# Clamping and shifting weight words in PSUM, and running the last group of a feed-forward layer by token block

## The chip, the cores and the metric

The kernel runs on one core of a Trainium2 chip. The time is the device time of one execution, in microseconds (us); the profile is that of one execution on the same core. Engines are named as in the profile: PE is TensorE's matmul (PEld its weight load), DVE is VectorE, ACT is ScalarE, POOL is GpSimd, SP is the engine whose queue issues the loads.

## The reference

Attention over 2 batches, 8 heads, 576 tokens and 64 dimensions a head, with rotary embedding and a softmax, and after it two feed-forward layers on 1152 tokens of 512 columns. The weights are float64.

```python
x = attention(rotate(q), rotate(k), v)         # 1152 x 512
h = np.maximum(x @ w_in, 0.0)                  # 512 x 2048
x = (h * h @ w_out).astype(np.float32)         # 2048 x 512
a = x @ w_a                                    # 512 x 1536
b = x @ w_b
out = (a * b @ w2_out).astype(np.float32)      # 1536 x 512
```

## The kernel before

**Attention.** Eight pairs of heads, nine blocks of queries each. A block's scores are made on PE (`emit_S`, line 202), their maximum on DVE, the exponential on ACT (`emit_exp`, line 217), then transposes and the product with V on PE. All eight PSUM banks are in use: pool `ps` has the tags `s` (two slots of two banks), `t` and `av` (two slots of one bank each). The last pair's product is evacuated when the feed-forward stage starts.

**Feed-forward stage.** A matmul in full float32 is made of three in a rounded format (`three`, lines 390 to 392): weight high part by activation high part, high by low, low by high. So every weight and every activation is split into a high part (a cast) and a low part (a subtraction). Tokens run in three blocks of 384 (`NTB`, `TB`). In the first layer 16 blocks of 128 hidden columns are taken in groups of four (`G`). `unit1(f, n)` makes block f for token block n: 12 matmuls into a PSUM bank, the relu on ACT (line 416), then `gated`: the product v on DVE (line 408, one operand in PSUM, one in SBUF), a cast on ACT (line 409), a subtraction on POOL (line 410). `out1(g, m, n)` sums a group's four blocks: 12 matmuls (they carry the lines 390 to 392 too, as y<-g,w_o), then an add into an accumulator on DVE, and for the last group a split of the result into `yb`, the input of the second layer. In the second layer `unit2` makes two products and gates them, `out2` sums them and stores.

PSUM results of this stage go round the three tags of `ps` in turn (`bank`, line 384): six banks, of each `s` slot only the first half.

**Weights.** `prep_weight` (line 63) is called for each of 68 weight blocks ahead of the first step that wants it. SP loads 512 float64 words a partition (`raw`, two slots). ACT scales the high words and bends negative ones (lines 75 and 76, into `cl`, two slots in SBUF). DVE shifts the low words right by 29 into `bits` (line 77), clamps `cl` (line 78), and shifts `cl` left by 3 and ors the two (line 79). `bits` (two slots in SBUF) is then the float32 weight. ACT casts it to the high part in `w` (line 81), POOL subtracts to make the low part (line 82). `w` has 14 slots, three of which lie outside of what attention occupies. Loads, casts and steps of later weights run ahead of their use as far as the slots allow.

**Order.** `steps` (line 475 on) lists the units: for the first group all four blocks by token block; then, for each group, the rest of its units by block f with n inside, the first block of the next group, and the sums. The last group's sums run by token block. Each engine runs its own instructions in an order fixed when the program is built, so the order within an engine need not be that of the code, but an instruction that waits holds all behind it on its engine.

Of the kernel before, what the change touches and what calls it, by code (L numbers as in the profile page):

```python
# [7 lines left out]
F32 = mybir.dt.float32  # L8
# [5 lines left out]
ALU = mybir.AluOpType  # L14
AX = mybir.AxisListType

P = 128
# [4 lines left out]
NTB = 3  # L22
KC = 4
NF1 = 16
NF2 = 12
G = 4
LT = 3
DM = 512
NWT = 14
NWA = 3  # L30
BANKS = ("t", "av", "s")


@with_exitstack
def attention_moe_moe2_kernel(ctx: ExitStack, tc: tile.TileContext, qk, rope, vm, vt, ident_in, sel_in, w_in, w_out, w_a, w_b, w2_out, out):
    nc = tc.nc
    act, dve, pool, pe = nc.scalar, nc.vector, nc.gpsimd, nc.tensor
# [6 lines left out]
    tmp = ctx.enter_context(tc.tile_pool(name="tmp", bufs=1))  # L44
# [8 lines left out]
    def psum_s(name):  # L53
        return ps.tile([P, 2, 512], F32, tag="s", name=name)

    def psum_1(tag, name):
        return ps.tile([P, 512], F32, tag=tag, name=name)
# [5 lines left out]
    def prep_weight(key):  # L63
        st = raw.tile([P, DM], I64, tag="raw", name=f"raw_{key[0]}{key[1]}")
        nc.sync.dma_start(out=st, in_=src_of[key[0]][key[1]])
        w = wpools[int(len(W) % NWT >= NWA)].tile([P, 2, DM], F32R, tag="w", name=f"w_{key[0]}{key[1]}")
        W[key] = w
        words = st.bitcast(I32).rearrange("p (n two) -> p n two", two=2)
        low = words[:, :, 0]
        highf = st.bitcast(F32).rearrange("p (n two) -> p n two", two=2)[:, :, 1]  # L70
        cl = tmp.tile([P, DM], F32, tag="cl", bufs=2, name=f"cl_{key[0]}{key[1]}")
        bits = tmp.tile([P, DM], I32, tag="bits", bufs=2, name=f"bits_{key[0]}{key[1]}")
        clb = cl.bitcast(I32)

        act.activation(cl, highf, AF.Copy, scale=REBIAS)
        act.activation(cl, cl, AF.Prelu, alpha=TURN)
        dve.tensor_scalar(out=bits, in0=low, scalar1=29, scalar2=None, op0=ALU.logical_shift_right)  # L77
        dve.tensor_scalar(out=cl, in0=cl, scalar1=-HI * TURN, scalar2=HI, op0=ALU.max, op1=ALU.min)
        dve.scalar_tensor_tensor(out=bits, in0=clb, scalar=3, in1=bits, op0=ALU.logical_shift_left, op1=ALU.bitwise_or)
        val = bits.bitcast(F32)  # L80
        act.copy(w[:, 0, :], val)
        pool.tensor_tensor(out=w[:, 1, :], in0=val, in1=w[:, 0, :].bitcast(F32), op=ALU.subtract)  # L82
# [1 line left out]
    src_of = {"i": w_in, "o": w_out, "a": w_a, "b": w_b, "2": w2_out}  # L84
    W = {}

    ps = ctx.enter_context(tc.tile_pool(name="ps", bufs=2, space=bass.MemoryType.PSUM))
    attn = ExitStack()
    a1 = attn.enter_context(tc.tile_pool(name="a1", bufs=1))
    a2 = attn.enter_context(tc.tile_pool(name="a2", bufs=2))  # L90
    pp = attn.enter_context(tc.tile_pool(name="pp", bufs=5))
# [254 lines left out]
    for i in range(NB + LT):  # L346
# [19 lines left out]
        if p + 1 < NPAIR:  # L366
            n = p + 1
# [11 lines left out]
    wpools.append(ctx.enter_context(tc.tile_pool(name="wb", bufs=NWT - NWA, reuse_waits="tile")))  # L379
    accp = ctx.enter_context(tc.tile_pool(name="accp", bufs=1, reuse_waits="tile"))  # L380

    banks = [0]

    def bank(name):
        tag = BANKS[banks[0] % len(BANKS)]
        banks[0] += 1
        return psum_s(name)[:, 0, :] if tag == "s" else psum_1(tag, name)

    def three(dst, wh, wl, mh, ml, first, last):
        pe.matmul(dst, wh, mh, start=first, stop=False)  # L390
# [21 lines left out]
    def unit1(f, n):  # L412
        h = bank(f"h{f}_{n}")[:, 0:TB]
        proj(h, W["i", f], xb[n])
        r = g2.tile([P, TB], F32, tag="r", name=f"r{f}_{n}")
        act.activation(r, h, AF.Relu)
        gated(("g", f), n, h, r, f"1_{f}")

    def unit2(f, n):
        a = bank(f"a{f}_{n}")[:, 0:TB]  # L420
        proj(a, W["a", f], yb[n])
        r = g2.tile([P, TB], F32, tag="r", name=f"s{f}_{n}")
        act.copy(r, a)
        b = bank(f"b{f}_{n}")[:, 0:TB]
        proj(b, W["b", f], yb[n])
        gated(("ab", f), n, b, r, f"2_{f}")
# [48 lines left out]
    steps = []  # L475
    N1, N2 = NF1 // G, NF2 // G
    steps += [(unit1, f, n) for n in range(NTB) for f in range(G)]
    for g in range(N1):
        if g:
            steps += [(unit1, g * G + f, n) for f in range(1, G) for n in range(NTB)]  # L480
        if g + 1 < N1:
            steps += [(unit1, (g + 1) * G, n) for n in range(NTB)]
        if g < N1 - 1:
            steps += [(out1, g, m, n) for m in range(KC) for n in range(NTB)]
        else:
            steps += [(out1, g, m, n) for n in range(NTB) for m in range(KC)]
    for g in range(N2):
        steps += [(unit2, g * G + f, n) for f in range(0 if g == 0 else 1, G) for n in range(NTB)]
        if g + 1 < N2:
# [3 lines left out]
    for fn, *a in steps:  # L493
        if fn is unit1:
            keys = [("i", a[0])]
        elif fn is unit2:
            keys = [("a", a[0]), ("b", a[0])]
        else:
            keys = [("o" if fn is out1 else "2", a[0] * G + k) for k in range(G)]
        for key in keys:  # L500
            if key not in W:
                prep_weight(key)
        fn(*a)
# [66 lines left out]
```

## Time and profile before

| what | us |
|---|---|
| median of 3 runs (628.09 to 630.75) | 628.31 |
| the profiled execution | 628.47 |
| its span in the trace | 626.7 |
| PE busy | 591.8 |
| DVE busy | 352.1 |
| ACT busy | 322.4 |
| POOL busy | 267.7 |

The span runs from the first to the last instruction of the profiled execution; a row's start is counted from the span's start. [...]

### The profile page before, as it was taken

To read this page: it belongs to the slowest core of one execution; us is meant where nothing else is said; L and a number is where in the kernel's file an instruction comes from. 1 tells how busy PE (TensorE), PEld (TensorE's weight loads), DVE (VectorE), ACT (ScalarE), POOL (GpSimd) and SP (SyncE) were. 2 spreads that over 40 slices of the span, in tenths; PEclk is the share of its full clock that TensorE was granted. 3 is DMA by queue.
4 is the path that set the end of the run, shared out by engine and by line. 5 is a ranking of instruction groups with operands and counts; after the bars stand their busy time and mean duration, and the time that the engine had idled before them with its cause. 6 is when DMAs were issued, how large, how long until landed. Compare 5 with 4: busy or idle time off the path is not lost.

```text
span 626.7 us, 8927 instructions
## 1 busy us (share of the span) xinstructions
PE 591.8 (94%) x3368; PEld 523.3 (84%) x3368; DVE 352.1 (56%) x550; ACT 322.4 (51%) x685; POOL 267.7 (43%) x278
## 2 busy tenths in 40 slices
PE   0699999999999979999999979999999999999998
PEld 0667665666659968999999979999998999889986
DVE  5977677765528894855766676653441545221122
ACT  2577776787646777652563464455534644102200
POOL 4557656622127772652653452344450454302210
PEclk9999999999999999999999999999999999999999
DMA  7665756562004442411421331142221421000012
GB/s 244 179 189 140 208 167 191 120 188 57 18 1 152 150 144 94 158 59 53 134 68 69 93 109 35 66 130 73 67 68 69 134 68 68 0 1 1 0 52 100
DMA packets 20678, 61.41 MB, mean 98 GB/s; under 512 B 3337, under 2 KB 3721, under 8 KB 19739
## 3 DMA queue, kind: packets, MB, share of 16 engines
q1 hardware_dynamic: 20635, 60.85, 31.6%
q8 instruction: 26, 0.43, 0.3%
q14 instruction: 17, 0.14, 0.1%
HBM read 48.16 MB, written 2.36 MB: 81 GB/s over the span
## 4 chain that ended last, share of the span: by engine, by line
PE 62%; DVE 12%; issue 9%; ACT 6%; DMA 5%; POOL 4%; SPq 0%; ACTq 0%; DVEq 0%; POOLq 0%
PE s L202 8%; PE av L314 7%; PE t L272 5%; PE a L392 4%; PE b L392 4%; PE a L390 4%; PE b L390 4%; PE a L391 4%; PE b L391 4%; PE o L466 4%; PE o L465 4%; PE o L464 4%; POOL w_i L82 2%; DVE bits_o L77 2%; PE y L391 1%
## 5 line engine op out<-in xcount | busy, mean ns | idle before, releaser
L410 POOL TENSOR_TENSOR g<-v,g 128x384 fp32r<-128x384 f32 x84 | 94.9, 1130 | 142.6 <-ACT g L409 140.2
L409 ACT CAST g<-v 128x384 fp32r<-128x384 f32 x84 | 42.8, 509 | 82.4 <-DVE v L408 82.1
L202 PE MATMUL s<-sk 128*128 128x288 f32 x336 | 66.0, 327 | 19.6 <-DVE sk L180 14.5
L202 PEld LDWEIGHTS s<-sk 128*128 128x128 f32 x336 | 49.8, 200 | 38.4 <-DVE sk L180 14.5
L390 PE MATMUL y<-g,w_o 128*128 128x384 f32 x192 | 65.7, 342 | 8.4 <-DVE v L408 4.0
L211 DVE TENSOR_REDUCE st<-s 128x1 f32<-128x576 f32 x72 | 53.7, 752 | 33.8 <-PE s L202 33.6
L391 PE MATMUL y<-g,w_o 128*128 128x384 f32 x192 | 65.0, 339 | 0.9 <-POOL g L410 0.9
L392 PE MATMUL y<-g,w_o 128*128 128x384 f32 x192 | 64.8, 338 | 0.0
L390 PE MATMUL h<-x,w_i 128*128 128x384 f32 x192 | 64.3, 335 | 0.2 <-DVE v L408 0.2
L392 PE MATMUL h<-x,w_i 128*128 128x384 f32 x192 | 64.1, 334 | 0.0
L391 PE MATMUL h<-x,w_i 128*128 128x384 f32 x192 | 64.1, 334 | 0.0
L217 ACT ACTIVATE P<-s,st 128x576 f32<-128x576 f32 x72 | 53.6, 745 | 11.9 <-DVE st L211 11.8
L314 PE MATMUL av<-PT,V 128*64 128x384 f32 (+1 forms) x256 | 53.1, 426 | 0.0
L272 PE MATMUL t<-ident,P 128*128 128x128 f32 x288 | 46.5, 285 | 1.7 <-DVE PT L257 1.5
L392 PE MATMUL a<-yb,w_a 128*128 128x384 f32 x144 | 48.1, 334 | 0.0
L390 PE MATMUL a<-yb,w_a 128*128 128x384 f32 x144 | 48.1, 334 | 0.0
L391 PE MATMUL a<-yb,w_a 128*128 128x384 f32 x144 | 48.1, 334 | 0.0
L390 PE MATMUL b<-yb,w_b 128*128 128x384 f32 x144 | 48.1, 334 | 0.0
L391 PE MATMUL b<-yb,w_b 128*128 128x384 f32 x144 | 48.1, 334 | 0.0
L392 PE MATMUL b<-yb,w_b 128*128 128x384 f32 x144 | 48.1, 334 | 0.0
L390 PEld LDWEIGHTS y<-g,w_o 128*128 128x128 f32 x192 | 36.4, 190 | 11.4 <-DVE v L408 5.6
L466 PE MATMUL o<-w,g 128*128 128x512 f32 (+1 forms) x112 | 42.8, 382 | 0.0
(118 smaller groups left out, 1345.7 us busy)
## 6 DMA issues: line engine op xcount, KB each, us to landing
raw_i<-in_w_in SPq DMA_DIRECT2D x16, 512.0 KB, 3.4
raw_o<-in_w_out SPq DMA_DIRECT2D x16, 512.0 KB, 3.3
X<-in_qk SPq DMA_DIRECT2D x7, 1152.0 KB, 5.4
raw_a<-in_w_a SPq DMA_DIRECT2D x12, 512.0 KB, 3.2
raw_b<-in_w_b SPq DMA_DIRECT2D x12, 512.0 KB, 3.4
raw<-in_w_out SPq DMA_DIRECT2D x12, 512.0 KB, 3.4
sk<-hi_lo SPq DMA_DIRECT2D x14, 432.0 KB, 5.7
sk<-hi_lo SPq DMA_DIRECT2D x14, 288.0 KB, 5.9
```

The costliest lines, as they stand in the source:

```text
L202: pe.matmul(s[:, b, c:c + n], lhs, rhs, start=(m < 2), stop=(m >= len(mm) - len(cuts)), skip_group_check=(j == 8))
L211: dve.tensor_reduce(out=ST[p][:, 0, j:j + 1], in_=SP[i][:, :, 0:288], op=ALU.max, axis=AX.XY, negate=True)
L217: act.activation(pr[:, h, :].rearrange("p (b n) -> p b n", b=2), SP.pop(i)[:, :, 0:288], AF.Exp, bias=st[:, 0, j:j + 1], scale=1.0, accum_ ...
L272: pe.transpose(t[:, k * P:(k + 1) * P], flat[:, c0:c0 + P], ident)
L314: pe.matmul(AVT[p, r][half(h), 0:n], V[p][:, h, k, :], PT[p][:, h, k, q0:q0 + n], start=False, stop=(k == 3), skip_group_check=True)
L390: pe.matmul(dst, wh, mh, start=first, stop=False)
L391: pe.matmul(dst, wh, ml, start=False, stop=False)
L392: pe.matmul(dst, wl, mh, start=False, stop=last)
L409: act.copy(gt[:, 0, c], val)
L410: pool.tensor_tensor(out=gt[:, 1, c], in0=val, in1=gt[:, 0, c].bitcast(F32), op=ALU.subtract)
L464: pe.matmul(dst, gt[:, 0, c], w[:, 0, d], start=(k == 0), stop=False)
L466: pe.matmul(dst, gt[:, 1, c], w[:, 0, d], start=False, stop=(k == G - 1))
```

## The change

Four edits. In `prep_weight` the tile `cl` moves to a PSUM pool `mps` (two slots, one bank each); the list `mps` is filled before the first call, so every weight takes that branch. The clamp is now followed by a shift of `cl` in place, and the last DVE step shifts the raw low words and ors them with `cl`; the early shift of the low words into `bits` is gone. The pool `ps` is closed with attention, and all results of the feed-forward stage come from one tag `m` of `mps`, six slots of one bank. The pool's tiles wait for the tiles that they overlap, not for the whole pool before them (`reuse_waits="tile"`). And in the first layer's last group the units and the sums alternate by token block: units of block 0, units of block 1, sums of block 0, units of block 2, sums of block 1, sums of block 2.

```diff
+        if mps:
+            cl = mps[0].tile([P, DM], F32, tag="cl", bufs=2, name=f"cl_{key[0]}{key[1]}")
+        else:
+            cl = tmp.tile([P, DM], F32, tag="cl", name=f"cl_{key[0]}{key[1]}")
         clb = cl.bitcast(I32)

         act.activation(cl, highf, AF.Copy, scale=REBIAS)
         act.activation(cl, cl, AF.Prelu, alpha=TURN)
-        dve.tensor_scalar(out=bits, in0=low, scalar1=29, scalar2=None, op0=ALU.logical_shift_right)
         dve.tensor_scalar(out=cl, in0=cl, scalar1=-HI * TURN, scalar2=HI, op0=ALU.max, op1=ALU.min)
-        dve.scalar_tensor_tensor(out=bits, in0=clb, scalar=3, in1=bits, op0=ALU.logical_shift_left, op1=ALU.bitwise_or)
+        dve.tensor_scalar(out=clb, in0=clb, scalar1=3, scalar2=None, op0=ALU.logical_shift_left)
+        dve.scalar_tensor_tensor(out=bits, in0=low, scalar=29, in1=clb, op0=ALU.logical_shift_right, op1=ALU.bitwise_or)
...
-    ps = ctx.enter_context(tc.tile_pool(name="ps", bufs=2, space=bass.MemoryType.PSUM))
+    mps = []
     attn = ExitStack()
+    ps = attn.enter_context(tc.tile_pool(name="ps", bufs=2, space=bass.MemoryType.PSUM))
...
+    mps.append(ctx.enter_context(tc.tile_pool(name="mps", bufs=6, space=bass.MemoryType.PSUM, reuse_waits="tile")))

     def bank(name):
-        tag = BANKS[banks[0] % len(BANKS)]
-        banks[0] += 1
-        return psum_s(name)[:, 0, :] if tag == "s" else psum_1(tag, name)
+        return mps[0].tile([P, 512], F32, tag="m", name=name)
...
-        if g:
+        if 0 < g < N1 - 1:
             steps += [(unit1, g * G + f, n) for f in range(1, G) for n in range(NTB)]
...
         else:
-            steps += [(out1, g, m, n) for n in range(NTB) for m in range(KC)]
+            for n in range(NTB + 1):
+                if n < NTB:
+                    steps += [(unit1, g * G + f, n) for f in range(1, G)]
+                if n:
+                    steps += [(out1, g, m, n - 1) for m in range(KC)]
```

## Rows read from the trace of the kernel before

**Rows 1.** The page, part 1: busy us (share of the span) xinstructions.

```profile
PE 591.8 (94%) x3368; PEld 523.3 (84%) x3368; DVE 352.1 (56%) x550; ACT 322.4 (51%) x685; POOL 267.7 (43%) x278
```

**Rows 2.** What PE waited for, whole span: us in total, times, longest.

```profile
PE s L202 <- DVE sk L180: 14.5, 1, 14.5
...
PE y L390 <- DVE v L408: 4.0, 4, 1.4
...
PE t L272 <- DVE PT L257: 1.5, 1, 1.5
```

**Rows 3.** Timeline of PE: start, duration (us), engine, line, operation, out<-in, count.

```profile
185.86 0.44 PE L390 MATMUL h<-x,w_i 128*128 128x384 f32 x1
...
190.13 0.33 PE L390 MATMUL h<-x,w_i 128*128 128x384 f32 x1
```

**Rows 4.** Timeline of PE; in brackets the idle time before, and its releaser.

```profile
222.09 0.44 PE L390 MATMUL y<-g,w_o 128*128 128x384 f32 x1 [1.45 <-DVE v L408]
```

**Rows 5.** Timeline of DVE and PE, 371 to 379 us.

```profile
371.13 1.21 DVE L77 TENSOR_SCALAR bits<-raw 128x512 int32<-128x512 int32 x1
...
372.99 0.55 DVE L408 TENSOR_TENSOR v<-h,r 128x384 f32<-128x384 f32 x1
...
374.19 0.44 PE L390 MATMUL y<-g,w_o 128*128 128x384 f32 x1 [2.88 <-ACT g L409]
...
375.27 0.69 PE L391 MATMUL y<-g,w_o 128*128 128x384 f32 x1 [0.64 <-POOL g L410]
...
378.25 0.34 PE L391 MATMUL y<-g,w_o 128*128 128x384 f32 x1
```

**Rows 6.** Busy time by window: PE, PEld, DVE, ACT, POOL, then granted clock PEclk.

```profile
376.00:378.00 2.00, 2.00 (x8) 2.00 (x8) 0.65 (x2) 2.00 (x5) 1.40 (x2) 0.50 0.00 0
```

**Rows 7.** Timeline of DVE: the stage's 14th v, the last group's third.

```profile
230.89 0.54 DVE L408 TENSOR_TENSOR v<-h,r 128x384 f32<-128x384 f32 x1
...
361.03 0.55 DVE L408 TENSOR_TENSOR v<-h,r 128x384 f32<-128x384 f32 x1
```

**Rows 8.** Busy time by window of the shift, L77: window, DVE busy (count), PEclk.

```profile
0.00:187.00 187.00, 2.08 (x5) 1.00 0.51 143
...
187.00:231.50 44.50, 14.78 (x13) 1.00 0.43 142
```

**Rows 9.** The same of the clamp, L78.

```profile
0.00:187.00 187.00, 2.90 (x7) 1.00 0.51 143
...
187.00:231.50 44.50, 6.39 (x10) 1.00 0.43 142
```

**Rows 10.** The same of the shift-and-or, L79.

```profile
0.00:187.00 187.00, 3.42 (x5) 1.00 0.51 143
...
187.00:231.50 44.50, 12.69 (x12) 1.00 0.43 142
```

**Rows 11.** The same of v, L408.

```profile
187.00:231.50 44.50, 7.67 (x14) 1.00 0.43 142
```

**Rows 12.** Groups by line and shape, whole span: busy us, mean ns, idle before.

```profile
L257 DVE COPY PT<-t 128x512 f32<-128x512 f32 x15 | 10.2, 683 | 2.9 <-PE t L272 2.9
```

**Rows 13.** Tile cl_i, to 190 us: ns min/median/max, first and last start us.

```profile
L75 ACT ACTIVATE cl_i<-raw_i x5: 668/672/683, 73.3 to 131.8; 128x512 f32<-128x512 f32 x5
...
L76 ACT ACTIVATE cl_i<-cl_i x5: 617/642/660, 74.3 to 133.4; 128x512 f32<-128x512 f32 x5
...
L78 DVE TENSOR_SCALAR cl_i<-cl_i x5: 396/411/422, 80.6 to 136.0; 128x512 f32<-128x512 f32 x5
```

**Rows 14.** Busy time by window of all engines: PE, PEld, DVE, ACT, POOL.

```profile
187.00:231.50 44.50, 40.09 (x225) 38.16 (x223) 39.14 (x49) 30.95 (x62) 34.17 (x28) 1.00 0.43 142
```

**Rows 15.** The page, part 6: DMA issues, count, KB, median us to landing.

```profile
raw_i<-in_w_in SPq DMA_DIRECT2D x16, 512.0 KB, 3.4
```

**Rows 16.** Timeline of ACT: end of the first score slot's last softmax.

```profile
169.45 0.20 ACT L217 ACTIVATION_READ_ACCUMULATOR P<-s,st 128x1 f32 x1
```

**Rows 17.** Timeline of POOL: the last w_in weight's low half.

```profile
300.25 1.29 POOL L82 TENSOR_TENSOR w_i<-bits_i,w_i 128x512 fp32r<-128x512 f32 x1 [12.75 <-ACT w_i L81]
```

More of the change, by code (lines that the diff above doesn't have):

```diff
@@ L30 @@
 NWA = 3
-BANKS = ("t", "av", "s")
 @with_exitstack
@@ L70, in prep_weight @@
         highf = st.bitcast(F32).rearrange("p (n two) -> p n two", two=2)[:, :, 1]
-        cl = tmp.tile([P, DM], F32, tag="cl", bufs=2, name=f"cl_{key[0]}{key[1]}")
         bits = tmp.tile([P, DM], I32, tag="bits", bufs=2, name=f"bits_{key[0]}{key[1]}")
+        if mps:
+            cl = mps[0].tile([P, DM], F32, tag="cl", bufs=2, name=f"cl_{key[0]}{key[1]}")
+        else:
+            cl = tmp.tile([P, DM], F32, tag="cl", name=f"cl_{key[0]}{key[1]}")
         clb = cl.bitcast(I32)
@@ L380, in attention_moe_moe2_kernel @@
     accp = ctx.enter_context(tc.tile_pool(name="accp", bufs=1, reuse_waits="tile"))
-    banks = [0]
+    mps.append(ctx.enter_context(tc.tile_pool(name="mps", bufs=6, space=bass.MemoryType.PSUM, reuse_waits="tile")))
     def bank(name):
-        tag = BANKS[banks[0] % len(BANKS)]
-        banks[0] += 1
-        return psum_s(name)[:, 0, :] if tag == "s" else psum_1(tag, name)
+        return mps[0].tile([P, 512], F32, tag="m", name=name)
     def three(dst, wh, wl, mh, ml, first, last):
```

## The prediction

> **What bounds the kernel now.** I read the busy table first, then what TensorE (PE) waited for, then the PE timeline where those waits lie. PE is busy for 94% of the span [rows 1], so the change can be worth only PE's idle time and what a lower clock costs. Of the 34.9 us between busy time and span, 14.5 us are the start, before the first scores [rows 2], and 8 us more lie in the first 40 us and behind the last matmul; the change reaches none of these. Attention keeps one stop of 1.5 us, at 99 us [rows 2]. The feed-forward stage begins at 185.86 us [rows 3] and has two places where PE stops. From 215 to 246 us there are eight stops, 5.5 us in all (the largest is shown) [rows 4]. [...] A stop of 0.41 us at 288 us is the rest; layer two has none.
>
> Place one, 215 to 231 us. A unit of the first layer is 12 matmuls: 24 of them lie between the two matmul rows, 4.27 us, so about 2.1 us a unit [rows 3]. VectorE (DVE) must make v for each before its bank comes free. The 14th v starts at 230.89 us [rows 7]; its unit's matmuls ended near 185.9 + 14 x 2.1 = 215 us, so DVE is 16 us late. Six banks cover five further units, some 10.4 us; beyond that PE stops. DVE is full there: in 44.5 us the shift took 14.78 us, the clamp 6.39, the shift-and-or 12.69 and v 7.67 [rows 8 to 11], 41.5 us together. The three weight steps are that long only beside GpSimd (POOL) work. Before 187 us, where POOL has little to do, a shift took 2.08/5 = 0.42 us, a clamp 0.41, a shift-and-or 0.68; in the stretch they took 1.14, 0.64 and 1.06 [rows 8 to 10]. The v step, one operand in PSUM and one in SBUF, took 0.55 us in the midst of it [rows 11].
>
> Place two, 371 us. The last group's first sum has used three of its four gated blocks and waits for the fourth, whose v started at 372.99 us, behind weight steps of the second layer such as the shift of 1.21 us at 371.13 [rows 5]. That block's unit is two units ahead of the group's last, which ended at 369.6 us, so it ended near 365.4: DVE was 7.5 us late.
>
> **Part 1: clamp and shift in PSUM.** Per weight three DVE steps stay three, and all follow the second ScalarE (ACT) step; the shift on the low word, which could run early, is gone. The trace has no clamp that writes PSUM. The nearest row is the copy of 512 columns out of PSUM, 0.68 us on DVE [rows 12]; the floor is the quiet clamp, 0.41 us [rows 9], and the ceiling 0.64 to 1.14 us, if the waits beside POOL stay. I take 0.68 for clamp and shift, because operand place and size match, and 0.69 for the last step, its quiet value: 2.05 us a weight, against 2.84 in the stretch and 1.51 in quiet. With at most one operand in SBUF these should behave like v, which POOL never stretched. In the stretch: 12 weights x 2.05 = 24.6, plus 2.7 us for what was done ahead of 187 us and now isn't (two clamps and most of the fifth weight), plus 7.7 for v: 35.0 us instead of 41.5. DVE would be 16 - 6.5 = 9.5 us late, just inside the 10.4 us that banks cover. So the five stops released by DVE go (4.0 us [rows 2] and a short one of 0.2); of the other three (1.3 us, ACT and POOL last) I count a quarter. Gain 4.5 us, bounds 0 and 5.5. On ACT the two steps go to PSUM instead of SBUF; they took 0.67 and 0.64 us [rows 13], and I count no change, since ACT is busy 31 of the 44.5 us [rows 14].
>
> [...]
>
> The raw words are now held to the third DVE step instead of the first, so the next load on SP's queue is issued later by about two steps. Nothing else is queued on SP after the last attention load. One round of a raw slot becomes landing 3.4 [rows 15], ACT 1.3 [rows 13], DVE 2.05, some hand-overs: 7.1 us, for two slots 3.55 us a weight; before, 12 weights took 44.5 us, 3.7 us each [rows 10]. PE needs the ninth weight at 217 us and the 17th at 267; counted from 170 us that is 5.2 and 5.7 us a weight. Cost zero while a weight takes less; above, 9 us for each us of excess.
>
> **Part 2: PSUM anew.** Six banks rotate for sums as before; two now hold clamped words. Before, five weights (the clamps at 80.6 to 136.0 us [rows 13]) were made inside attention. Now none can be until attention gives banks back. I assume that slots are laid out in the order of first request, so that the two clamp slots fall on the first score slot, read last by the softmax that ended at 169.65 us [rows 16]; which slot it is the trace doesn't say. Then weight i0 is whole at 169.7 + 1.3 + 2.05 + 0.6 + 1.3, about 175 us, i1 at 177.5, i2, after its load, at 182.5 and i3 at 187; PE wants them at 185.9, 188, 190 and 192. Cost 0.5 us (0 to 2) for their ACT and DVE steps between attention's last ones. Inside attention, the steps that leave free some time: a shift of 0.42 us [rows 8] stands on DVE in the queue ahead of the 1.5 us stop [rows 2]. Gain 0.4 (0 to 1.5).
>
> **Part 3: the last group by token block.** PE's work is the same. The first sum now starts after six units instead of nine, and needs the third unit, not the seventh. With the lateness of before, that unit's v came at 361.0 us [rows 7]; behind v come a cast on ACT and POOL's subtraction, which at place two let the matmul start 2.3 us after v did (372.99 to 375.27 [rows 5]), so about 363.5. The sum wants it at about 365. Afterwards each block's sums (4 x 2.1 = 8.3 us of PE) stand between its last unit and its use. So both stops go, 2.88 + 0.64 us [rows 5]. And the clock: from 375.27 to 378.25 us [rows 5] nine matmuls took 2.98 us instead of 9 x 0.178 = 1.6, so 1.4 us more. Together 4.9 us (bounds 3 and 4.9). The three w_in weights are wanted within 6 us, not 19; the last of them was whole at 301.6 us [rows 17]. Their slots come free 5 to 17 us later, which delays three second-layer weights to about 376 us; PE needs those after 430.
>
> **Sum.** 628.3 - 4.5 - 4.9 - 0.4 + 0.5 = 619.0 us. The profiled execution took 628.47 us with a span of 626.7, the median is 628.31, so differences in the trace count one to one.
>
> **Rivals.**
> *Only part 3 pays.* DVE is relieved, but ACT or POOL (34 of 44.5 us busy [rows 14]) is late in its place, and the stops at 215 to 246 us stay: 628.3 - 4.9 = 623.4. For it: three stops there were released by those two. Against: these are the short ones. 0.15.
>
> *Clamp slots come free only at attention's end.* If the two banks are read until 186.4 us, i0 is ready for PE at 190.4, i2, whose load then starts at 189.8, at 197.3, and i3 at 199.4 instead of 192: 7.3 us lost, and about 1.4 us for the clock that such a stop cost at 374 us. 619.0 + 8.7 = 627.7, no change. 0.11.
>
> [...] 0.06.
>
> *Slower: weights are late.* Raw words, clamped words and bits have two slots each, all held longer. If one weight at a time goes round, 7.1 us each, the ninth comes at 170 + 64 = 234 instead of 217 us, 17 us late, and the 32nd at 397 instead of 386 plus those 17, no further loss. 619.0 + 17 = 636. It decides from 6.3 us a weight on, where 9 us eat the gain. Against it the pace of 3.7 us before. With orders on the engines that turn out worse in some such way, 0.12.
>
> **How the numbers follow.** The forecast, 616.5 to 622, has 0.56; the rivals 0.15, 0.11, 0.06 and 0.12. Up to 628 leaves out the last and the third; below 616.5 all stops of the feed-forward stage and the one in attention would have to go. Range 616.5 to 628. A measurement of this kernel tells 0.5%, 3.1 us, from no change: faster is below 625.2. Forecast and first rival with it 0.72 (0.71 and a little of the second), within 0.5% 0.16, slower 0.12.
>
> **What would show it.** Clamp and shift at 0.65 to 0.7 us each, the same beside POOL and away from it; no PE stop above 0.3 us between 210 and 246 us after the same count of units; no stop and no clock below 1.00 in the last group; the first feed-forward matmul within 1 us of 185.9, and no PE wait on a weight's ACT cast behind it. Wrong would be: DVE steps above 0.9 us, first clamps after 180 us, PE waiting for a weight's high or low half, or a new stop where the first block's sums begin.

## The result, and the profile after

| kernel (same chip) | median, us | runs, us | ratio to before, 95% interval |
|---|---|---|---|
| before | 628.85 | 628.09 to 630.75 | |
| changed | 621.0 | 620.45 to 622.08 | 0.9873 [0.9845, 0.9901] |

The change is worth 7.9 us; 9.3 were predicted, and 621.0 lies within the range. The profiled execution took 620.49 us with a span of 618.7, 7.98 us less than that of before. Two terms of the sum were far off, though, in opposite directions. That shows in the trace before any experiment.

The page of the changed kernel, part 1 (compare [rows 1]), and two of its costliest groups (line, engine, operation, out<-in, count, busy and mean ns, idle before). All lines of the weight and gating code lie one to three higher than before: copy L77, prelu L78, clamp L79, shift L80, last step L81, v L409.

```profile
PE 584.4 (94%) x3368; PEld 521.7 (84%) x3368; DVE 333.9 (54%) x550; ACT 322.1 (52%) x685; POOL 255.2 (41%) x278
...
L411 POOL TENSOR_TENSOR g<-v,g 128x384 fp32r<-128x384 f32 x84 | 85.3, 1018 | 136.7 <-ACT g L410 129.9
...
L391 PE MATMUL h<-x,w_i 128*128 128x384 f32 x192 | 65.5, 341 | 7.3 <-ACT w_i L83 7.3
```

What PE waited for in the changed kernel, whole span: us in total, times, longest (compare [rows 2]).

```profile
PE s L205 <- DVE sk L183: 15.0, 1, 15.0
PE h L391 <- ACT w_i L83: 7.3, 2, 6.2
PE s L205 <- ACT P L220: 5.4, 3, 4.0
PE r L250 <- DVE rows L260: 1.2, 2, 1.0
PE h L393 <- POOL w_i L84: 1.1, 2, 0.7
PE t L275 <- DVE PT L260: 0.8, 1, 0.8
```

The waits of sums on v [rows 2], at 222 us [rows 4] among them, and those on the cast and the subtraction behind a late v at 374 us [rows 5] are gone. In their place stands a wait that the kernel before didn't have: PE waits for the first weights of the feed-forward stage.

The timeline of ACT, DVE and PE there (start, duration, engine, line, operation, out<-in, count; in brackets the idle time before, and its releaser).

```profile
163.14 0.75 ACT L220 ACTIVATE P<-s,st 128x576 f32<-128x576 f32 x1
...
178.15 0.60 ACT L333 CAST x<-xf 128x192 fp32r<-128x192 f32 x2 [2.85 <-DVE xf L330]
...
180.76 0.35 ACT L333 CAST x<-xf 128x192 fp32r<-128x192 f32 x1 [1.22 <-DVE xf L330]
181.01 1.16 ACT L77 ACTIVATE cl_i<-raw_i 128x512 f32<-128x512 f32 x2
182.12 1.03 ACT L78 ACTIVATE cl_i<-cl_i 128x512 f32<-128x512 f32 x2
...
182.69 1.30 DVE L79 TENSOR_SCALAR cl_i<-cl_i 128x512 f32<-128x512 f32 x2 [1.97 <-ACT cl_i L78]
...
186.47 0.69 PE L391 MATMUL h<-x,w_i 128*128 128x384 f32 x1 [6.21 <-ACT w_i L83]
...
187.82 0.69 PE L393 MATMUL h<-x,w_i 128*128 128x384 f32 x1 [0.34 <-POOL w_i L84]
...
195.16 0.45 PE L391 MATMUL h<-x,w_i 128*128 128x384 f32 x1 [1.09 <-ACT w_i L83]
...
196.52 0.44 PE L393 MATMUL h<-x,w_i 128*128 128x384 f32 x1 [0.74 <-POOL w_i L84]
```

Attention's last product ended at 180.26 us, 5.7 us sooner than the 185.93 of before. But no weight was ready: the first two copies stand on ACT directly behind the cast of attention's last result. Which banks the two clamp slots took no trace shows; if it was the first score slot, as the prediction assumed, the softmax at 163.14 us was the last to read it. ACT then stood idle several times (2.85 us ahead of 178.15), but the copy came behind all of attention's steps in its order, without idle time of its own before it. So I read it as ACT's order, and not a bank still in use, that held the copy. That is argued and not shown: no run placed the copy earlier with the words still in PSUM. One run speaks for it: with the words in SBUF, in a pool that opens only behind attention (below), no bank is wanted, and the first copy started at 180.77 us all the same. The two first weights also went through each step as a pair (x2 in the rows), so that the first one's three DVE steps took from 182.69 to about 185.8 us instead of some 2.05 us.

The windows of the changed kernel behind that stop: PE, PEld, DVE, ACT, POOL busy, PE's granted clock (1.00 is the full clock), DMA share, GB/s.

```profile
180.30:186.40 6.10, 0.00 (x0) 0.00 (x0) 4.03 (x7) 2.99 (x7) 0.59 (x1) 0.67 0.00 0
186.40:200.00 13.60, 11.36 (x45) 10.03 (x46) 5.48 (x9) 7.40 (x15) 7.01 (x6) 0.77 0.45 154
...
186.40:192.30 5.90, 5.49 (x16) 4.98 (x17) 0.98 (x2) 2.70 (x6) 2.50 (x2) 0.50 0.50 178
192.70:200.00 7.30, 5.48 (x29) 4.65 (x29) 4.10 (x7) 4.32 (x9) 4.51 (x4) 1.00 0.44 144
...
200.00:217.00 17.00, 17.00 (x100) 17.00 (x99) 12.59 (x22) 14.54 (x31) 13.06 (x12) 1.00 0.36 125
```

PE did 45 matmuls in 13.6 us, while the next 17 us hold 100. In those 13.6 us are three stops, 2.17 us; most of the rest of the loss is the clock, which was granted at 0.50 up to about 192.5 us and at 1.00 from there on: matmuls start 0.32 us apart in the first part, 0.17 in the second. 19 pairs of matmuls start over 0.23 us apart without a stop between them, 2.9 us more than at the usual 0.17; 16 of the pairs and 2.6 us lie in the half-clock part, and the other three pairs behind it.

The DVE steps of the weights in the changed kernel, windows by line: L79 (clamp), L80 (shift), L81 (last step), each 187 to 231.5 us (DVE busy and count, granted clock), then all engines in that stretch (compare [rows 8 to 11, 14]).

```profile
187.00:231.50 44.50, 7.47 (x11) 0.94 0.42 141
...
187.00:231.50 44.50, 6.95 (x10) 0.94 0.42 141
...
187.00:231.50 44.50, 6.83 (x10) 0.94 0.42 141
...
187.00:231.50 44.50, 42.34 (x227) 41.03 (x226) 27.77 (x46) 32.71 (x66) 29.68 (x27) 0.94 0.42 141
```

A step takes 0.68 to 0.70 us beside POOL, and as long elsewhere: over all 68 weights the clamp and the shift stayed at 0.69 to 0.70 us, the last step at 0.67 to 0.69. In the stretch the weight steps took 21.2 us of DVE and v 8.3 us, against 33.9 and 7.7 [rows 8 to 11]; 31 weight steps fell into it instead of 35. DVE now keeps up: the 14th v, which started some 16 us behind its unit's last matmul before [rows 7], starts 0.9 us behind it (PE, then DVE).

```profile
221.21 0.33 PE L393 MATMUL h<-x,w_i 128*128 128x384 f32 x1
...
222.40 0.56 DVE L409 TENSOR_TENSOR v<-h,r 128x384 f32<-128x384 f32 x1 [1.15 <-POOL g L411]
```

DVE is busy 27.8 us in the stretch instead of 39.1, and POOL's subtraction of the gated blocks takes 1.02 us on average instead of 1.13.

Cut at four points, the two profiled executions compare as follows (us).

| stretch | before | after | difference | predicted |
|---|---|---|---|---|
| to the first scores | 14.54 | 15.01 | +0.47 | 0 |
| first scores to the end of attention's last product | 171.39 | 165.25 | -6.14 | -0.4 |
| from there to the first feed-forward matmul | -0.07 | 6.21 | +6.28 | +0.5 |
| first to last feed-forward matmul | 437.75 | 429.16 | -8.59 | -9.4 |

The rest of both executions is equal to 0.01 us, so the four rows add up to -7.98. The first row is not the change's: across the runs below it moved between 14.5 and 15.2 us. Each stretch is that of one profiled execution; kernels that do the same inside attention differ there by up to 1.0 us (the table further down).

### The profile page after: what moved, and what is told of

It reads as the page before. It is cut to its first block, busy times and chain, and to the rows that moved or that the text cites. A ratio compares the mean times of both kernels' runs of the same rounds, so it can differ in the third digit from the quotient of the medians.

```text
span 618.7 us, 8930 instructions
## 1 busy us (share of the span) xinstructions
PE 584.4 (94%) x3368; PEld 521.7 (84%) x3368; DVE 333.9 (54%) x550; ACT 322.1 (52%) x685; POOL 255.2 (41%) x278
## 4 chain that ended last, share of the span: by engine, by line
PE 91%; DVE 5%; ACT 1%; DMA 1%; issue 1%; POOL 0%; SPq 0%; DVEq 0%; ACTq 0%
PE s L205 8%; PE av L317 7%; PE h L393 6%; PE h L391 5%; PE h L392 5%; PE y L391 5%; PE y L392 5%; PE y L393 5%; PE t L275 5%; PE a L392 4%; PE b L392 4%; PE a L393 4%; PE b L393 4%; PE a L391 4%; PE b L391 4%; PE o L467 4%
## 5 line engine op out<-in xcount | busy, mean ns | idle before, releaser
L411 POOL TENSOR_TENSOR g<-v,g 128x384 fp32r<-128x384 f32 x84 | 85.3, 1018 | 136.7 <-ACT g L410 129.9
L205 PEld LDWEIGHTS s<-sk 128*128 128x128 f32 x336 | 48.5, 195 | 40.3 <-ACT P L220 15.0
L391 PE MATMUL h<-x,w_i 128*128 128x384 f32 x192 | 65.5, 341 | 7.3 <-ACT w_i L83 7.3
L393 PE MATMUL h<-x,w_i 128*128 128x384 f32 x192 | 65.5, 341 | 1.1 <-POOL w_i L84 1.1
L392 PE MATMUL h<-x,w_i 128*128 128x384 f32 x192 | 65.1, 339 | 0.0
L391 PE MATMUL y<-g,w_o 128*128 128x384 f32 x192 | 64.1, 334 | 0.0
L392 PE MATMUL y<-g,w_o 128*128 128x384 f32 x192 | 64.1, 334 | 0.0
L393 PE MATMUL y<-g,w_o 128*128 128x384 f32 x192 | 64.1, 334 | 0.0
L220 ACT ACTIVATE P<-s,st 128x576 f32<-128x576 f32 x72 | 53.6, 745 | 11.3 <-DVE st L214 11.1
L317 PE MATMUL av<-PT,V 128*64 128x384 f32 (+1 forms) x256 | 48.0, 425 | 0.0
L409 DVE TENSOR_TENSOR v<-b,s 128x384 f32<-128x384 f32 x36 | 19.9, 553 | 50.3 <-PE b L393 50.3
L391 PEld LDWEIGHTS h<-x,w_i 128*128 128x128 f32 x192 | 36.9, 192 | 8.0 <-ACT w_i L83 8.0
```

Source lines behind the costliest of these rows:

```text
L205: pe.matmul(s[:, b, c:c + n], lhs, rhs, start=(m < 2), stop=(m >= len(mm) - len(cuts)), skip_group_check=(j == 8))
L220: act.activation(pr[:, h, :].rearrange("p (b n) -> p b n", b=2), SP.pop(i)[:, :, 0:288], AF.Exp, bias=st[:, 0, j:j + 1], scale=1.0, accum_ ...
L317: pe.matmul(AVT[p, r][half(h), 0:n], V[p][:, h, k, :], PT[p][:, h, k, q0:q0 + n], start=False, stop=(k == 3), skip_group_check=True)
L392: pe.matmul(dst, wh, ml, start=False, stop=False)
L393: pe.matmul(dst, wl, mh, start=False, stop=last)
L409: dve.tensor_tensor(out=val, in0=src, in1=other, op=ALU.mult)
```

## The experiments

Three questions: which part pays in the feed-forward stage; why attention ended sooner, where PE showed no idle time; and what the stop at its end costs once it is taken away.

**Part 3 alone.** The kernel before with the new order of the last group.

```diff
-        if g:
+        if 0 < g < N1 - 1:
             steps += [(unit1, g * G + f, n) for f in range(1, G) for n in range(NTB)]
...
-            steps += [(out1, g, m, n) for n in range(NTB) for m in range(KC)]
+            for n in range(NTB + 1):
+                if n < NTB:
+                    steps += [(unit1, g * G + f, n) for f in range(1, G)]
+                if n:
+                    steps += [(out1, g, m, n - 1) for m in range(KC)]
```

> The kernel before with the last group by token block alone. Theory (the stop at 371 us comes from the seventh unit's late v, and the new order needs only the third): both stops of the last group (2.88 + 0.64 us) and the 1.4 us of half clock behind them go, the eight stops at 215 to 246 us (5.5 us) stay; 628.3 - 4.9 = 623.4 us, 622.5 to 624.5. Rival (VectorE is so late there that the first block's sums now stop instead): 626 to 629 us, with a PE stop of over 1 us where those sums begin.

624.39 us (624.19 to 624.59) against 629.26, ratio 0.992 [0.9902, 0.9939]: the 4.9 us of the prediction. In its timeline no stop is left in the last group, while those from 220 to 241 us stay.

```profile
223.70 0.44 PE L390 MATMUL y<-g,w_o 128*128 128x384 f32 x1 [1.44 <-DVE v L408]
...
233.12 0.44 PE L390 MATMUL y<-g,w_o 128*128 128x384 f32 x1 [1.33 <-DVE v L408]
```

**Parts 1 and 2 alone.** The changed kernel with the old order of the last group (that diff turned round).

> The changed kernel with the old order of the last group. Theory (clamp and shift in PSUM take VectorE's waits beside GpSimd away everywhere): VectorE is relieved in the last group too, but by less than the 7.5 us that it was late; stops of 0 to 2 us there, 621 to 623.5 us against 621.0. Rival (only the order helps there, VectorE's weight steps in PSUM do not): the stops of 3.5 us and the half clock come back, 625.5 to 626.5 us.

621.63 us (620.33 to 623.07), ratio 0.9877 [0.985, 0.9904], not to be told from the change as a whole. In its profiled execution, the longest of the four, the clock fell a second time, behind the stops near 197 us, which cost some 1.8 us (mean granted clock 0.989; 0.992 and 0.994 in the two executions of under 621 us). What PE waited for in this kernel, all of it but two rows of the start:

```profile
PE h L391 <- ACT w_i L83: 7.3, 2, 6.2
...
PE r L250 <- DVE rows L260: 1.2, 2, 1.0
PE h L393 <- POOL w_i L84: 1.1, 2, 0.7
PE t L275 <- ACT PT L258: 0.2, 1, 0.2
```

No sum waits for v, in the last group either: the v that held the sum at 374 us started 3.2 us behind its unit here, and 7.4 before. So part 3 is worth 4.9 us to the kernel before and nothing, within the error, once the words are in PSUM: DVE was late in the last group for the same reason as at 215 us. The gains of the two parts are one gain there, not two.

**The words in SBUF again.** The changed kernel, new DVE steps and new order included, with `cl` back in SBUF.

```diff
-        if mps:
+        if False:
             cl = mps[0].tile([P, DM], F32, tag="cl", bufs=2, name=f"cl_{key[0]}{key[1]}")
         else:
-            cl = tmp.tile([P, DM], F32, tag="cl", name=f"cl_{key[0]}{key[1]}")
+            cl = tmp.tile([P, DM], F32, tag="cl", bufs=2, name=f"cl_{key[0]}{key[1]}")
```

> The changed kernel with the clamped words in SBUF again (two slots), the new sequence of VectorE steps and the new order kept. Theory (the stops at 215 to 246 us came from weight steps stretched beside GpSimd, and weights made inside attention slow it): weight steps of 0.7 to 1.2 us on average in that stretch, PE stops of 4 to 6 us come back, the stop of 6.2 us before the feed-forward stage is gone, attention ends near 186 us instead of 180.3; 622 to 625 us. Rival (the stops at 215 to 246 us are gone because fewer weights are made there, or because the early shift is gone, not because of PSUM): no such stops, 616 to 619 us.

630.24 us (10 runs, 628.31 to 631.74), ratio 1.0015 [1.0, 1.0031]: the whole gain is gone, more than the theory wanted. Its DVE steps by window, L79, L80 and L81, each in 0 to 180 us and in the stretch of the table (in the kernel before POOL was busy for 88.4 of the first 187 us, and for 34.2 of the stretch's 44.5); then the first of its late stops.

```profile
0.00:180.00 180.00, 3.48 (x7) 1.00 0.53 148
187.00:231.50 44.50, 6.46 (x8) 1.00 0.33 107
...
0.00:180.00 180.00, 2.94 (x7) 1.00 0.53 148
187.00:231.50 44.50, 7.90 (x8) 1.00 0.33 107
...
0.00:180.00 180.00, 3.77 (x5) 1.00 0.53 148
187.00:231.50 44.50, 9.45 (x10) 1.00 0.33 107
...
261.99 0.44 PE L391 MATMUL h<-x,w_i 128*128 128x384 f32 x1 [2.08 <-DVE v L409]
```

Up to 180 us the clamp takes 0.50, the shift 0.42 and the last step 0.75 us on average; in the stretch 0.81, 0.99 and 0.95, that is 2.7 us a weight against 2.05 in PSUM. That it is POOL's company shows step by step: over the whole of this trace the 41 shifts that no POOL instruction overlaps took 0.41 to 0.43 us each, the 27 others 1.03 on average; in the kernel before it was 0.41 to 0.43 for 22 and 1.24 on average for 46; in the changed kernel both kinds take 0.70. The stops of the feed-forward stage came to 8.6 us, 9.4 before; only some 2.3 us of them lie between 215 and 246 us, where the theory had 4 to 6, and most lie later, from 262 to 294 us, and are released by v. The rival falls: 8 to 10 weights went through the stretch here, no more than in the changed kernel, and yet the 14th v was 10.7 us late, and the 20th 14.7. Attention lasted 171.81 us, as before, and there was no stop behind it. So the place of the words decides, and the new steps and order without it give nothing.

**The words in SBUF, but late.** Is it PSUM's layout or the weights' leaving that lets attention end sooner? The kernel before, with `cl` in an SBUF pool that is opened after attention.

```diff
-        cl = tmp.tile([P, DM], F32, tag="cl", bufs=2, name=f"cl_{key[0]}{key[1]}")
+        cl = late[0].tile([P, DM], F32, tag="cl", name=f"cl_{key[0]}{key[1]}")
...
     wpools.append(ctx.enter_context(tc.tile_pool(name="wb", bufs=NWT - NWA, reuse_waits="tile")))
+    late.append(ctx.enter_context(tc.tile_pool(name="late", bufs=2, reuse_waits="tile")))
```

> The kernel before, but the clamped words lie in an SBUF pool that opens only when attention is closed, so that no weight is made inside attention; VectorE's steps, PSUM and order as before. Theory (a weight made inside attention costs PE about 0.8 us there; seven in part or whole cost 5.7): attention's last matmul ends near 180.3 us instead of 186, then PE stops for 5 to 7 us for the first weight and again for the third and fourth; the stops at 215 to 246 us stay in part, since weights come later; 626 to 632 us. Rival (attention ended sooner for the PSUM pool's sake, by another order of its own matmuls): attention ends near 186 us and the stop for the first weight comes on top, 631 to 637 us.

636.15 us (635.84 to 636.41), ratio 1.0105 [1.0083, 1.0128], above the theory's range and inside the rival's; the profile has to decide. The profiled execution took 1682.54 us and is left out here; the kernel ran once more for a profile.

> The kernel before with the clamped words in an SBUF pool that opens only when attention is closed, looked at again for its profile. Theory (the seven weights made in whole or part inside attention are what slows attention there): its last product matmul ends near 180.5 us, then PE stops for 5 to 7 us for the first weight, and later stops by VectorE remain. Rival (the new PSUM pool let attention end sooner): the last product matmul ends near 186 us.

636.3 us, a single run. Attention lasted 166.91 us instead of 171.39 with its PSUM pool untouched, and its last product ended at 181.6 us: it is the weights' leaving. The stop for the first weight was 3.3 us, not 5 to 7. Yet the kernel is some 7 us slower than before: the weights that were made inside attention are now due behind it, and PE waits longer for v, for casts and for weights than before. What its PE waited for, the rows of the feed-forward stage above 1 us:

```profile
PE y L392 <- DVE v L410: 4.8, 6, 1.5
PE h L392 <- ACT w_i L81: 3.3, 1, 3.3
PE y L392 <- ACT g L411: 2.9, 1, 2.9
PE y L392 <- ACT yacc L443: 1.9, 2, 1.7
PE h L394 <- POOL w_i L82: 1.9, 2, 1.2
```

**Three first weights in SBUF.** The changed kernel, in which only the first weights keep their words in SBUF, so that they can be made inside attention.

```diff
-        if mps:
+        if len(W) > 3:
             cl = mps[0].tile([P, DM], F32, tag="cl", bufs=2, name=f"cl_{key[0]}{key[1]}")
```

> The changed kernel, but the first three weights have their clamped words in SBUF and may be made inside attention; all others stay in PSUM. Theory (each weight inside attention costs PE 0.8 to 1.6 us there, and the stop ahead of the feed-forward stage, 6.2 + 2.2 us and 2.9 us of half clock, comes from the first weights alone): attention ends near 184 us, no stop of over 1 us behind it, 612 to 615.5 us. Rival (other waits, for the last pair's product, end the stop no sooner): 618 to 621 us, PE still idle for over 4 us before the first feed-forward matmul.

615.71 us (615.51 to 616.25), ratio 0.9791 [0.9775, 0.9808], just over the expected range. The stop of 6.2 us and the half clock are gone, but the fourth weight, the first with its words in PSUM, was late by 1.15 and 0.39 us, where no stop of over 1 us was expected:

```profile
192.98 0.44 PE L391 MATMUL h<-x,w_i 128*128 128x384 f32 x1 [1.15 <-ACT w_i L83]
```

Attention lasted 170.33 us: three weights cost 5.1 of the 6.1 us that leaving them out had gained.

**The first group by weight block.** The changed kernel with the first group's units by block f, token block inside, so that the second weight is wanted three units later, not one.

```diff
-    steps += [(unit1, f, n) for n in range(NTB) for f in range(G)]
+    steps += [(unit1, f, n) for f in range(G) for n in range(NTB)]
```

> The changed kernel with the first group's units by weight block instead of token block, so that each of the first four weights is used for three units, 6.2 us, before the next is wanted; words in PSUM as in the change. Theory (the stops of 1.09 and 0.74 us and part of the slow clock at 187 to 200 us come from the third and fourth weight, wanted 2.1 us apart): the stop of 6.2 us stays, those go, 617 to 619.5 us. Rival (the order by token block was needed for the last pair's product, which the second and third token block contain): a new stop of over 1 us in the second or third unit, 621 us or more.

618.25 us (617.74 to 619.47), ratio 0.9833 [0.9818, 0.9847]. As expected, the two stops at 195 us are gone; the first one stays (6.22 us), and the clock behind it cost 2.5 us. So in the changed kernel PE stood still there (1.09 and 0.74 us) with units behind in its order that were ready: here units of the first weight for later token blocks ran before 195 us without a stop.

**Both, with one weight, and with a third raw slot.** The changed kernel with two edits, `len(W) > 1` in place of `mps` as the condition and the order by weight block; then the same with `bufs=3` for `raw`.

> Both: the first weight alone has its clamped words in SBUF and may be made inside attention, and the first group runs by weight block. Theory: attention ends near 181.5 us, no stop of over 1 us behind it, the other weights have 6.2 us each, 609.5 to 612.5 us, below both kernels. Rival (one weight inside attention changes attention's order as much as seven did): attention ends near 184 to 186 us, 614 to 617 us.

> The kernel that keeps the first weight's clamped words in SBUF and runs the first group by weight block, with a third slot for raw words. Left over in the run of that kernel were two stops at the start of the feed-forward stage, 1.15 us at 190.33 us and 0.40 us, where PE waits for the second weight; the third weight's load was issued late there because both raw slots were held. Theory: what holds the second weight is the order of ACT (its first step stands behind attention's last), not its raw words, so the stop of 1.15 us stays within 0.3 us and only the third weight's steps come earlier: 613.5 to 614.5 us. Rival: raw slots set the pace of the first weights; then both stops go, 1.5 us less: 612.5 to 613.0.

The first took 614.43 us (613.45 to 614.95), ratio 0.9767 [0.9753, 0.9782], 2 us over the expected range and in the rival's, though attention ended at 182.7 us, sooner than the rival had it (184 to 186) and later than the theory (181.5). The second weight is late by 1.15 and 0.40 us, and the low half of a later one by 0.60. The second took 613.23 us (612.9 to 614.05), ratio 0.9727 [0.9696, 0.9758], on another chip, and the time lies between theory and rival; its list of waits decides (the two rows of the feed-forward stage are shown). The stops of the second weight are the same, so its raw words weren't what held it; only the later stop of 0.60 us is gone.

```profile
PE h L391 <- ACT w_i L83: 1.1, 1, 1.1
PE h L393 <- POOL w_i L84: 0.4, 1, 0.4
```

**Both, with two weights.** The same two edits with `len(W) > 2`.

> As the kernel with one weight's clamped words in SBUF and the first group by weight block, but with two weights in SBUF. Attention ended at 180.3 us with none inside it, 182.7 with one, 185.4 with three and 185.9 with five. Theory: each weight made inside attention costs its end about 2 us, so it ends at about 184.5; the stops of 1.15 and 0.40 us go: 614.4 + 1.8 - 1.5, 614.0 to 615.5 us, no better than one weight. Rival: the cost of the second is under 0.8 us, and the stops' 1.5 us come as gain: 612.5 to 613.7.

611.75 us (610.99 to 612.22), ratio 0.9701 [0.9663, 0.9739], the best of all; beside the kernel with a third raw slot, on the same chip, 1.5 us less. That is below the rival's range. The second weight lengthened attention by 0.9 us (168.82 against 167.87), nearer to the rival; the feed-forward stage lost all its stops and took 423.48 us, 2.1 less; and this run's first scores came 0.5 us sooner, which is chance. Its PE waits, all but that for the first scores:

```profile
PE s L205 <- ACT P L220: 5.2, 3, 4.0
PE r L250 <- DVE rows L260: 1.4, 2, 1.0
PE t L275 <- DVE PT L260: 1.3, 1, 1.3
PE t L275 <- ACT PT L258: 0.2, 1, 0.2
```

Nothing behind 120 us stops PE in this kernel, and the granted clock is 1.00 in the stage.

## Why the prediction came out as it did

**Part 1, the steps: right.** 0.68, 0.68 and 0.69 us were taken, 0.69 to 0.70 and 0.67 to 0.69 measured, the same beside POOL. The quiet steps of before were faster for clamp and shift [rows 8, 9], those beside POOL slower in all but the clamp [rows 8 to 10], and the stretch is what counts. A clamp of 0.41 us in quiet became one of 0.70 with its words in PSUM. It still didn't cost time: all three new steps took from 0.67 to 0.70 us everywhere, while with the words in SBUF the shift took 0.42 us up to 180 us and 0.99 in the stretch. That they read at most one operand from SBUF, as the prediction argued from v, doesn't explain it alone: in the kernel before, the shift and the clamp read one operand too, from SBUF, and took 1.24 and 0.83 us on average where a POOL instruction overlapped them, 0.42 and 0.42 where none did. What differs is the place of the words.

**Part 1, the stops: right, a little low, but DVE's lateness was mis-sized.** 4.5 of 5.5 us were to go; all eight stops went, and the one at 288 us too. The prediction had DVE still 9.5 us late, just inside what the banks cover; the 14th v was 0.9 us late. Of the forecast 35.0 us for weight steps and v in the stretch, 29.5 were measured (21.2 and 8.3), because 31 weight steps fell into it and not the 36, and what had been done ahead, that the sum counted. The first rival (ACT or POOL late instead) fell: ACT was busy 32.7 and POOL 29.7 of the 44.5 us, and neither stopped PE beyond the first weights.

**Part 2, the start: wrong.** "Cost 0.5 us (0 to 2)" was 6.21 us of stop, 2.17 us of further stops and 2.9 us for the clock, 11.3 us. The step that failed is the one from the slots' lying on the first score slot to weight i0's being whole at about 175 us: its first copy started at 181.01 us and PE got it at 186.47. When a bank is free says only when a step may run; where the step stands in ACT's order was taken for granted. Whether the order alone held the copy, or a bank too, isn't shown. The clamps ran from 182.69 us, behind the 180 that the prediction named as the sign of its being wrong. The second rival came near in size (7.3 + 1.4 us against 8.4 of stops and 2.9): weights did start only at attention's end, whether by its mechanism (banks read until then) or by ACT's order. Its time, 627.7, wasn't reached, for the next reason.

**Part 2, attention: wrong in size.** "Gain 0.4 (0 to 1.5)" was 6.1 us. The prediction asked only for idle time that PE showed, and PE showed 1.5 us there [rows 2]. The cost of the weights inside attention is no idle time in the records. One window of the kernel before, then the same of the changed kernel:

```profile
100.00:120.00 20.00, 20.00 (x125) 12.97 (x123) 14.12 (x28) 14.81 (x37) 11.69 (x15) 1.00 0.60 166
...
100.00:120.00 20.00, 19.76 (x136) 14.00 (x135) 15.04 (x25) 14.38 (x36) 11.48 (x15) 1.00 0.58 150
```

PE counts as busy all the time in the first, and yet does 11 matmuls fewer. Matmul records overlap (one of 0.33 us every 0.17 us), so short waits between them need not show; work done by a given time does. The runs give the price by the number of weights whose first ACT step lay inside attention, one profiled execution each.

| weights begun inside attention | attention, first scores to last product, us |
|---|---|
| 0 (changed; old order; by weight block) | 165.25; 165.95; 165.82 |
| 1, in its last 0.8 us (late in SBUF) | 166.91 |
| 1 (one weight; with third raw slot) | 167.74; 167.87 |
| 2 | 168.82 |
| 3 | 170.33 |
| 7 (before; part 3 alone; words in SBUF) | 171.39; 172.41; 171.81 |

Up to three, each costs some 1 to 2.5 us; seven cost some 6, little more than three. Whether it is ACT's time, DVE's, or the order in which PE got its scores and products stays open: PE's order inside attention differs between these kernels too, and no run held it fixed.

**Part 3: right alone, not as a term of this sum.** 4.9 us by itself, as predicted, and about none on top of part 1. The prediction costed both with the lateness of before. Part 1 had already shortened the weight steps that stood ahead of v at 373 us [rows 5].

**The sum.** So that 619.0 was near 621.0 is in part luck, since errors cancel: -6.1 instead of -0.4, +11.3 instead of +0.5, and within the feed-forward stage, without the stops and the clock of its start, some 13.7 us gained (8.59 + 2.17 + 2.9) instead of 9.4. Of these 13.7 us, 9.44 are the old stops, all of them; the rest, some 4.2, is longer times from one matmul's start to the next without a stop, of which the prediction counted 1.4 for the half clock at 375 us (granted 0.50 [rows 6]). The fourth rival (weights late throughout) fell: behind 197 us no weight was late. The third (0.06), DVE's weight steps slower than taken, fell: they took 0.67 to 0.70 us.

## What to carry over

Where an engine's steps are slowed by a neighbour, the place of the operands can be worth more than a short time in quiet (here 0.70 us everywhere for the shift in PSUM, against 0.42 away from POOL's work and 0.99 beside it in SBUF): compare the step's time in the place and company where it will run. When two parts of a change relieve the same late engine, cost the second with the first already done. When work moves across a stage's boundary, ask where it stands in the order of each engine, and measure the stage it leaves by work done by a given time and not by idle time; here two weights left on the old side, with the first group by weight block, were worth some 9 us more than moving all of them (611.75 against 621.0 us, though on different chips; 0.9701 and 0.9873 of the kernel before).

## What was not expected of the hardware

- In a window of attention in which PE showed 20.00 of 20 us busy it did 125 matmuls; in the same window of the kernel that makes no weights there it did 136.
- After a stop of 6.2 us the granted clock was 0.50 for the next 6 us and 1.00 from about 192.5 us on; with the stop taken away (one, two or three first weights in SBUF) its mean over the profiled execution was 0.999 to 1.000. The two shorter stops that followed (1.09 and 0.74 us) left it at 1.00 in the changed kernel, while in the profiled execution with the old order the same two were followed by a granted clock of 0.53 from 197.5 to 201.1 us.
- POOL's subtraction of gated blocks, which the change doesn't touch, took 1130 ns on average before and 1018 in the changed kernel. Before:

```profile
L410 POOL TENSOR_TENSOR g<-v,g 128x384 fp32r<-128x384 f32 x84 | 94.9, 1130 | 142.6 <-ACT g L409 140.2
```
